# A gated conv FFN behind block-causal attention: the first step of decoding the weights moves to ScalarE, its clamp then reads adjacent words, and the whole order is written anew

## Chip, cores and metric

One core of a Trainium2 chip. The metric is the device time of one execution in microseconds; lower is better. Three runs of the kernel before gave 648.29, 649.46 and 650.03 us (median 649.46).

## What is computed

For 8 batches, 8 heads, 576 positions and a head width of 64, attention with a mask by blocks of 64 positions, and behind it an FFN with a 3-tap convolution along the sequence that gates its own hidden layer. The weights arrive as float64 and are handed to the kernel as pairs of 32-bit words.

```python
scores = q @ k.T / 8, masked where pos_i // 64 < pos_j // 64
attn = exp(scores - max); attn /= sum(attn) + 1e-9
x = (attn @ v), heads side by side                # [8, 576, 512]
h = maximum(x @ w_in, 0)                          # w_in 512 x 1024
conv_out = conv_w[0]*h[t-1] + conv_w[1]*h[t] + conv_w[2]*h[t+1]
out = (h * sigmoid(conv_out)) @ w_out             # w_out 1024 x 512
```

## The kernel before

Everything is one program for one core, without loops at run time. The functions do not issue instructions where they stand: each calls `pl.op(engine, length, function, target, deps, bufs, other=...)`, which only notes an operation, its planned length and, in `other`, further engines that could do it. There are 3677 such operations. At the end `Plan.order` is given the numbers of `TARGETS`, one for each operation in the order of their creation: a number divided by 4 is the operation's place in its engine's queue, and its remainder by 4 chooses the engine (0 the first way, 1 to 3 one of `other`). `order` then walks through a model of the five engines with the planned lengths and settles two more things by it: which of the eight PSUM banks a tile gets, and where TensorE is given filler matmuls (`work`, L1775 in the profile) because its planned idle time is longer than 0.4 us. What runs on the chip is therefore a fixed queue for each engine; nothing is chosen at run time, and an engine that waits holds everything behind it in its queue.

The work has two parts. In the first, batch 0 is computed in two passes over the queries (A: positions 0 to 255, B: the rest), with scores by f32 matmuls (`stage_sa`, L1334, and `stage_sb`, L1273), row maxima on VectorE (L1352, L1289), exponentials on ScalarE (L1360, L1292), the division by the row sum on GpSimd (`norm`, L1375 for 128 and 256 columns, L1310 for 384 and 512), transposes on TensorE (`stage_x`, L1408), their copies out of PSUM on ScalarE (L678) and the product with v (`stage_pv`, L1452). At the same time the weights are loaded and decoded: 16 blocks of 128 x 512 (`load_w`, 8 of w_in and 8 of w_out) and one of 24 x 128 (`load_conv`). In the second part the batches 1 to 7 follow, with attention by `stage_s` (scores L1109, maxima L1208, exponentials L1211, planes L1058 to L1080, product L1492) while the FFN of the batch before runs (`ffn`: first product L1545, relu L1564, taps L1570 to L1587, tanh L1590, gate L1593, planes L1597 to L1604, second product L1638, scaling L1648 and store L1656).

`decode` turns the pairs of words of a float64 into a float32 and is what the change edits. A raw tile holds the words as [128, 512, 2], so word 1, `words(1)`, of neighbouring numbers lies 8 bytes apart, while the result `g` is adjacent. Its four steps are

```python
s1: g = min(words(1) * 2**-112, limit)               # GpSimd or VectorE, L884
s2: words(0) = words(0) >> 29                        # VectorE, L889
s3: words(0) = (words(1) & sign) | words(0)          # VectorE, L892
s4: g = (g << 3) | words(0)                          # VectorE, L897, needs s1 and s3
```

`load_w` calls it with `pool` true for blocks 1 to 15, so that s1 is planned on GpSimd with `c_pool(512) + 0.05`, which is 0.64 us; block 0 and the taps have s1 on VectorE. Behind `decode` come the block's maximum (L921 on VectorE before, for w_in; L924 on ScalarE behind, for w_out), the common scale (`scale_w`, `sums`) and the split into two f16 planes (`split_w`, L952 to L961). The loads of the blocks are issued by SyncE, in its queue among those of q, k and v.

In `Plan.order` a result of one engine reaches an operation of another one `DRAIN + SIGNAL` later (VectorE to VectorE: 0.08 us, the drain alone, before the change).

Of the kernel before, what the change touches and what calls it, by code (L numbers as in the profile page):

```python
# [21 lines left out]
0 12 8 4 0 16 20 8 4 28 24 32 60 80 129 84 196 68 81 64 77 252 128 88 272 284 300 12 36 20 32 60 12 40 18 40 48 0 12 4 8 16 24 44 92 56 100 104 128 72  # L22
204 80 168 184 192 52 120 60 108 156 288 92 244 108 224 248 264 76 208 100 176 260 292 108 268 136 316 324 412 128 320 152 396 416 428 328 336 348 356
368 176 140 388 400 408 420 424 276 472 268 436 197 480 185 516 288 528 189 520 324 560 316 588 144 204 548 616 624 444 132 200 456 488 500 332 140
208 580 596 604 440 156 216 536 556 608 432 160 240 564 696 756 548 184 276 684 700 708 508 172 232 620 644 792 576 180 268 764 784 796 580 816 316
512 820 828 836 844 325 848 616 880 612 864 604 872 628 892 624 896 608 860 600 852 4 56 28 48 32 68 36 44 20 84 88 52 48 40 44 28 24 72 16 52 48 184
304 0 40 56 64 60 52 44 28 48 124 132 68 72 88 84 32 36 120 44 124 68 216 352 8 136 92 96 104 80 112 76 116 212 232 132 124 120 116 26 104 200 84 168
112 220 380 52 240 196 280 204 220 172 236 180 344 364 172 180 168 164 36 36 88 148 264 136 248 160 280 460 452 916 196 200 204 208 212 216 328 364
576 584 420 632 257 653 164 168 172 180 184 188 296 300 524 552 368 568 245 248 220 224 236 240 244 248 348 352 572 600 416 612 436 252 252 256 260
268 272 280 408 464 664 692 492 704 504 288 284 288 292 300 304 308 388 428 628 636 452 648 460 272 320 324 328 332 336 340 396 448 656 660 472 676  # L30
281 284 344 364 368 372 376 380 424 512 736 744 536 760 313 801 384 388 392 396 404 412 468 476 712 720 516 740 544 304 600 608 612 616 620 624 632
636 680 217 348 352 20 112 64 116 68 140 148 96 76 28 152 88 144 84 180 188 92 104 32 160 164 172 100 108 200 216 112 73 56 116 60 132 64 136 76 156
148 80 160 40 96 72 144 92 96 188 372 100 308 208 312 212 332 340 156 160 56 228 140 256 164 276 296 148 144 124 384 392 404 256 260 440 448 192 64
104 120 132 240 120 228 176 312 304 192 308 128 244 116 224 228 232 340 532 152 432 292 444 284 492 508 224 228 108 360 236 376 252 464 496 220 212
156 468 504 512 336 344 540 544 236 194 112 124 316 392 276 360 348 404 400 360 412 296 376 264 356 400 408 456 668 144 484 384 476 372 592 640 260
264 456 728 520 732 524 748 752 296 300 416 680 672 688 496 500 716 724 292 140 148 152 432 488 480 552 468 528 532 472 540 420 480 496 564 504 508
596 840 440 444 448 572 580 584 636 644 912 924 684 940 696 368 516 520 524 532 536 568 648 660 920 936 700 964 373 376 424 428 436 548 552 556 877
656 904 928 688 944 361 364 484 488 492 604 640 644 708 720 984 988 732 1000 385 1013 452 460 464 540 560 564 640 728 996 1004 736 1016 393 396 312
352 356 576 588 628 668 712 976 980 724 992 381 388 528 592 596 648 652 656 704 740 1024 1028 748 1044 401 404 660 664 668 672 676 684 716 744 1040
1048 760 1064 772 440 728 732 740 744 748 756 768 772 832 840 700 704 708 716 720 724 776 780 1157 253 688 692 696 792 796 800 804 808 876 361 448 444  # L40
96 153 100 177 136 233 176 381 768 320 544 856 868 948 344 884 16 20 0 476 776 556 788 568 772 560 780 572 712 1036 756 1032 752 1052 1056 500 808 592
804 584 812 588 824 832 328 336 340 412 416 420 408 428 432 424 793 436 1062 1072 765 1068 665 960 332 908 240 228 232 4 768 1080 236 274 168 164 824
928 1284 633 888 12 24 8 680 968 808 972 780 1020 804 1008 788 760 1128 820 1124 828 1148 1152 736 1096 800 1084 796 1076 784 1116 1120 813 825 456
464 1186 484 460 849 1177 468 476 1201 853 1204 845 1196 817 1136 452 1144 272 264 268 473 1208 276 322 192 196 836 964 1344 653 900 788 1216 892 1180
868 1172 884 1220 896 784 1164 888 1168 880 905 1244 764 1160 856 1140 860 1132 836 1188 1192 488 492 496 917 1266 520 1254 921 512 508 925 516 504
1260 1270 1288 873 1236 865 1212 292 280 288 952 1316 296 308 224 220 848 1028 1428 933 1348 188 485 200 621 204 673 208 677 932 356 752 1088 1100
1104 816 1272 936 1248 944 1280 948 1276 940 828 1312 960 1304 956 1328 1332 812 1228 900 1224 912 1232 908 1256 1292 524 528 532 1342 548 552 1374
556 1381 969 973 544 540 1368 536 1360 1302 1324 1298 1308 308 300 312 1004 1396 316 778 244 248 876 1068 1464 1092 952 956 880 884 888 892 896 900
1088 1092 1500 1096 592 1112 1516 1125 1529 860 864 872 904 908 912 1497 1100 1508 1104 596 1120 1524 604 608 852 856 868 916 920 924 1505 1108 1512
1116 600 1132 1532 1542 616 928 932 936 940 944 948 1521 1136 1536 1128 612 1156 1560 1570 1581 952 956 960 964 968 972 1144 1148 1556 1152 620 1172  # L50
1588 1193 628 980 984 988 992 996 1000 1565 1184 1608 1176 632 1212 1624 640 1641 1004 1008 1012 1016 1020 1024 1188 1196 1612 1200 636 1216 1636 644
676 1056 1060 1064 1068 1072 1076 1665 1256 1688 1252 680 1276 1712 1281 684 1032 1036 1040 1100 1108 1112 1128 1132 1304 401 1048 1052 1088 1092 1096
1124 1144 1148 1340 417 1152 1156 1160 1164 1168 1172 1176 1180 1372 429 1200 1204 1208 1212 1216 1220 1224 1236 1961 461 1228 1232 1244 1248 1252
1256 1260 1264 1464 485 977 1404 840 1364 1008 1376 1012 1400 1020 1356 1000 832 1388 1016 1320 996 1412 1416 820 1336 980 1352 984 1240 988 993 1384
# [77 lines left out]
3336 3340 3344 3348 3352 3536 3540 4460 4468 3552 4476 1813 1816 3356 3360 3364 3368 3380 3384 3556 3560 4484 3564 1820 3576 4492 3581 1828 3448 3452  # L132
3456 3460 3464 3468 3596 3604 4516 4524 3608 4532 4538 4541 3424 3428 3432 3436 3440 3444 4501 3592 4504 4508 3600 4512 4522 4529 3416 3420 3488 3528
3532 3540 3548 3564 4549 1028 3480 3484 3496 3500 3504 3508 3524 3544 4545 1024 3472 3476 3512 3516 3552 3556 3560 3588 3612 1032 3404 3408 3412 3536
3568 3576 3584 3596 3616 3621 3492 3572 3580 3604 3608 3612 3636 3640 3628 3633 3520 3592 3600 3616 3620 3624 3628 3632 3624 1036
"""


# [1730 lines left out]
```

## Time and profile before

| | |
|---|---|
| median of three runs | 649.46 us (648.29 to 650.03) |
| the profiled execution, its own time | 652.3 us |
| span of its instructions | 650.5 us |
| mean granted TensorE clock over the span | 0.982 of full |
| busy share: TensorE, VectorE, ScalarE, GpSimd | 93%, 85%, 74%, 59% |

The profiled execution is 2.8 us above the median of the runs, and 1.8 us of its time lie outside the span. Busy time of TensorE contains stretches at half the clock and the fillers, so a busy TensorE is not always one that gets on with the work. Times of day in the profile are microseconds from the start of the span.

### The profile page before, as it was taken

Reading aid. Unit: us, or ns where it says so; the run is one execution under the profiler, and the core shown is the slowest. Engines: PE = TensorE matmul, PEld = TensorE weight load, DVE = VectorE, ACT = ScalarE, POOL = GpSimd, SP = SyncE. Lnnn points to the kernel's source line nnn. Section 1 sums busy time; section 2 is a strip of 40 time slices with the busy share of each in tenths; the row PEclk is TensorE's granted clock in tenths of the full one; section 3 lists DMA queues with packets and bytes.
Section 4 is the critical chain, followed back from the end, with each engine's and each line's share of the span. In section 5 each row is a group of like instructions: output and inputs, shape, how many; then the busy total and the mean of one; then the engine's idle time right before and its main releaser. Section 6 shows DMA issues by size and latency. Waiting matters only on the chain. (4 is left out here: it accounts for less than half of the span.)

```text
span 650.5 us, 15481 instructions
## 1 busy us (share of the span) xinstructions
PE 606.0 (93%) x5813; PEld 375.1 (58%) x5813; DVE 552.9 (85%) x1148; ACT 481.2 (74%) x1223; POOL 383.3 (59%) x465
## 2 busy tenths in 40 slices
PE   7787889988999999999999999999998999999997
PEld 5444645345874557645674557555755567566654
DVE  7689789999799998999989898989989896974850
ACT  4687789788797967998798676778877667972631
POOL 4978764665277524995587536873677445751320
PEclk9689889999999999999999999999999999999999
DMA  8744213399945999479984599359946662486002
GB/s 300 284 158 158 87 41 98 58 257 195 223 110 140 221 198 173 94 164 213 218 191 78 130 237 226 102 122 208 195 90 142 150 138 59 86 132 154 1 1 81
DMA packets 205503, 96.19 MB, mean 148 GB/s; under 512 B 185308, under 2 KB 187636, under 8 KB 205428
## 3 DMA queue, kind: packets, MB, share of 16 engines
q1 hardware_dynamic: 203844, 92.59, 63.7%
q10 hardware_dynamic: 1584, 2.62, 1.4%
q8 instruction: 45, 0.74, 0.5%
q14 instruction: 30, 0.25, 0.1%
HBM read 39.87 MB, written 9.44 MB: 76 GB/s over the span
## 5 line engine op out<-in xcount | busy, mean ns | idle before, releaser
L1638 PE MATMUL banks<-woh,shared 128*128 128x512 f16 (+1 forms) x592 | 183.5, 374 | 3.1 <-DVE t L1593 1.2
L1545 PE MATMUL banks<-x,wih 128*128 128x288 f16 (+2 forms) x1024 | 158.8, 289 | 8.0 <-DVE t L1593 2.1
L1638 PEld LDWEIGHTS <-shared 128*128 128x128 f16 x888 | 82.7, 98 | 110.1 <-issue 22.4
L1545 PEld LDWEIGHTS <-wih 128*128 128x128 f16 x1024 | 98.5, 99 | 42.5 <-issue 15.1
L1208 DVE TENSOR_REDUCE su<-banks 128x1 f32<-128x384 f32 (+8 forms) x252 | 110.1, 476 | 2.2 <-PE banks L1109 1.7
L1638 PE MATMUL banks<-wol,shared 128*128 128x512 f16 (+1 forms) x296 | 110.5, 373 | 0.0
L1587 POOL TENSOR_TENSOR t<-t,shared 128x575 f32<-128x575 f32 x51 | 75.2, 1477 | 53.5 <-DVE t L1574 50.4
L1109 PE MATMUL banks<-k,q 64*64 64x64 f32 (+7 forms) x1120 | 88.8, 415 | 7.6 <-DVE x L1503 2.8
L1545 PE MATMUL banks<-x,wil 128*128 128x288 f16 (+2 forms) x512 | 86.7, 288 | 0.0
L1604 POOL TENSOR_TENSOR shared<-t,shared 128x576 f16<-128x576 f32 (+2 forms) x53 | 65.4, 1237 | 17.8 <-ACT shared L1597 10.6
L1492 PEld LDWEIGHTS <-vb 128*64 128x64 f16 x1848 | 61.7, 111 | 11.1 <-issue 11.0
L1109 PEld LDWEIGHTS banks<-k,q 64*64 64x64 f32 x1120 | 38.7, 132 | 43.1 <-issue 10.6
L1574 DVE SCALAR_TENSOR_TENSOR t<-banks,cwb,t 128x575 f32<-128x575 f32 (+2 forms) x72 | 53.4, 742 | 10.5 <-ACT t L1570 6.6
L1590 ACT ACTIVATE t<-t 128x576 f32<-128x576 f32 (+2 forms) x72 | 45.1, 630 | 20.1 <-POOL t L1587 13.5
L1593 DVE SCALAR_TENSOR_TENSOR t<-t,banks 128x576 f32<-128x576 f32 (+2 forms) x72 | 48.8, 680 | 11.5 <-ACT t L1590 10.8
L1545 PEld LDWEIGHTS <-wil 128*128 128x128 f16 x512 | 49.8, 98 | 15.1 <-issue 1.7
L1570 ACT ACTIVATE t<-banks,cwb 128x576 f32<-128x576 f32 (+2 forms) x72 | 48.9, 682 | 7.6 <-DVE banks L1567 3.4
L1211 ACT ACTIVATE p3f<-banks,su 128x512 f32<-128x512 f32 (+1 forms) x56 | 36.7, 659 | 9.0 <-DVE su L1208 7.6
L1583 ACT ACTIVATE shared<-banks,cwb 128x575 f32<-128x575 f32 x51 | 37.5, 735 | 4.7 <-DVE banks L1567 4.0
L1211 ACT ACTIVATE p2f<-banks,su 128x320 f32<-128x320 f32 (+1 forms) x56 | 30.9, 554 | 11.0 <-DVE su L1208 9.8
L1648 ACT ACTIVATE stage<-banks,osc 128x512 f32<-128x512 f32 (+1 forms) x29 | 19.3, 669 | 25.3 <-PE banks L1638 23.1
L1564 ACT ACTIVATE banks<-banks 128x576 f32<-128x576 f32 (+2 forms) x50 | 28.1, 565 | 12.7 <-PE banks L1545 12.3
(202 smaller groups left out, 1199.2 us busy)
## 6 DMA issues: line engine op xcount, KB each, us to landing
vn<-in_v_dram SPq DMA_DIRECT2D x32, 320.0 KB, 3.8
q<-in_q_dram SPq DMA_DIRECT2D x28, 320.0 KB, 3.6
k<-in_k_dram SPq DMA_DIRECT2D x28, 320.0 KB, 3.6
out_dram<-stage SPq DMA_DIRECT2D x26, 256.0 KB, 3.2
shared<-in_moe_w_in_dram SPq DMA_DIRECT2D x8, 512.0 KB, 6.9
shared<-in_moe_w_out_dram SPq DMA_DIRECT2D x8, 512.0 KB, 3.4
out_dram<-stage ACTq DMA_DIRECT2D x9, 256.0 KB, 3.4
q<-in_q_dram SPq DMA_DIRECT2D x4, 192.0 KB, 5.6
```

The costliest lines, as they stand in the source:

```text
L1109: nc.tensor.matmul(out[64 * y:64 * y + 64], t["q"].ap[64 * r:64 * r + 64, q0:q0 + 64], t["k"].ap[64 * r:64 * r + 64, k0:k0 + c1 - c0], sta ...
L1208: nc.vector.tensor_reduce(out=st.ap[:, k:k + 1], in_=home[hh].ap[:, x], op=ALU.max, axis=AX.X, negate=True)
L1211: nc.scalar.activation(out=y.ap[:, 0:n], in_=home[hh].ap[:, x], func=AF.Exp, bias=st.ap[:, k:k + 1], accum_out=st.ap[:, 9 + k:10 + k])
L1492: nc.tensor.matmul(y, vb.ap[:, w, c, j, :], x, start=first, stop=(z == 1 and c == jobs[-1][0]), skip_group_check=True)
L1545: nc.tensor.matmul(h(a, z), wt[:, c, fs], xs[c][xi].ap[:, x0 + a:x0 + z], start=(n + c - c0 == 0), stop=(n + c - c0 == 3 * NCC - 1))
L1570: nc.scalar.activation(out=t.ap[:, 0:no], in_=h(own, own + no), func=AF.Copy, scale=cwb.ap[:, NFC + f:NFC + f + 1])
L1574: nc.vector.scalar_tensor_tensor(out=t.ap[:, i0:no], in0=h(own + i0 - 1, own + no - 1), scalar=cwb.ap[:, f:f + 1], in1=t.ap[:, i0:no], op0 ...
L1587: nc.gpsimd.tensor_tensor(out=t.ap[:, 0:i1], in0=t.ap[:, 0:i1], in1=u.ap[:, 0:i1], op=ALU.add)
L1590: nc.scalar.activation(out=t.ap[:, 0:no], in_=t.ap[:, 0:no], func=AF.Tanh)
L1593: nc.vector.scalar_tensor_tensor(out=t.ap[:, 0:no], in0=t.ap[:, 0:no], scalar=1.0, in1=h(own, own + no), op0=ALU.add, op1=ALU.mult)
L1604: eng.tensor_tensor(out=g[1][:, f, carry:carry + no], in0=t.ap[:, 0:no], in1=g[0][:, f, carry:carry + no], op=ALU.subtract)
L1638: nc.tensor.matmul(fb.ap[:, 0:cut], g[a][:, f, cs], w[:, f, ds], start=(f == 0 and n == 0), stop=(f == NFC - 1 and n == 2))
```

## The change

`decode` gets a step s0 ahead of s1, on ScalarE: it reads the words 8 bytes apart, multiplies by 2**-112, takes the absolute value and writes `g`. s1 then works on `g` in place, on adjacent words, as a clamp: a minimum with the limit and a maximum with 0. All 17 calls of `decode` have the same form, with s1 on GpSimd or, as the other way, on VectorE. In `Plan.order` the wait between two operations of one engine other than TensorE gets `SIGNAL` added (VectorE 0.035, ScalarE 0.035, GpSimd 0.08 us). And all of `TARGETS` is replaced: 3694 numbers, 17 more than before, found by a search with six sets of lengths.

```diff
-    def decode(words, g, n, at, deps, bufs, pool):
+    def decode(words, g, n, at, deps, bufs):
+        def s0():
+            nc.scalar.activation(out=g(), in_=words(1).bitcast(F32), func=AF.Abs, scale=2.0 ** -112)
         def s1(eng=nc.gpsimd):
-            eng.tensor_scalar(out=g(), in0=words(1).bitcast(F32), scalar1=2.0 ** -112, scalar2=2.0 ** -96 * (1 + 0x6FFFFF / 2.0 ** 23),
-                              op0=ALU.mult, op1=ALU.min)
+            eng.tensor_scalar(out=g(), in0=g(), scalar1=2.0 ** -96 * (1 + 0x6FFFFF / 2.0 ** 23), scalar2=0.0, op0=ALU.min, op1=ALU.max)
...
-        dv = (DVE, c_dve(n, True), partial(s1, nc.vector), True)
-        a = pl.op(POOL, c_pool(n) + 0.05, s1, at, deps=deps, bufs=bufs, other=(dv,)) if pool else \
-            pl.op(dv[0], dv[1], dv[2], at, deps=deps, bufs=bufs, port=True)
+        a = pl.op(ACT, c_act(n, False) + 0.035, s0, at, deps=deps, bufs=bufs)
+        a = pl.op(POOL, c_pool(n) + 0.05, s1, at, deps=[a], bufs=bufs, other=((DVE, c_dve(n, True), partial(s1, nc.vector), True),))
...
-                lat = self.DRAIN[e] + (self.SIGNAL[c.eng] if c.eng != e else 0.0) if (e != PE or c.eng != PE) else 0.0
+                lat = self.DRAIN[e] + self.SIGNAL[c.eng] if e != PE or c.eng != PE else 0.0
...
-        o = decode(words, lambda: g.ap, 512, at, [ld], [raw, g], f > 0)
+        o = decode(words, lambda: g.ap, 512, at, [ld], [raw, g])
...
-        o = decode(lambda w: raw.ap[:, :, w], lambda: g.ap, P, CONV + 1, [ld], [raw, g], False)
+        o = decode(lambda w: raw.ap[:, :, w], lambda: g.ap, P, CONV + 1, [ld], [raw, g])
```

By the remainders of the new numbers, 476 operations run on another engine than before. Up to batch 0's FFN it is 32 of 755, and VectorE's queue there gets 3 operations longer, ScalarE's 15 longer (17 of them s0), while GpSimd's keeps its 95. From batch 1 on it is 444 of 2922: VectorE has 30 operations fewer, GpSimd 24 more, ScalarE 13 more, and 7 stores fewer are issued by SyncE. s1 is on GpSimd for all 16 blocks of weights, and on VectorE for the taps.

## Rows read from the trace of the kernel before

**Rows 1.** The page, part 1: busy time and share of the span, instructions.

```profile
PE 606.0 (93%) x5813; PEld 375.1 (58%) x5813; DVE 552.9 (85%) x1148; ACT 481.2 (74%) x1223; POOL 383.3 (59%) x465
```

**Rows 2.** Stretches: length, busy PE, PEld, DVE, ACT, POOL, clock, DMA share, GB/s.

```profile
0.00:16.00 16.00, 12.67 (x77) 8.88 (x77) 12.29 (x42) 7.33 (x26) 7.29 (x21) 1.00 0.88 298
16.00:36.00 20.00, 13.18 (x78) 7.97 (x80) 14.03 (x37) 13.98 (x44) 19.15 (x20) 0.74 0.65 238
36.00:60.00 24.00, 22.26 (x165) 13.23 (x166) 21.57 (x64) 21.07 (x59) 18.81 (x20) 0.93 0.55 184
60.00:72.00 12.00, 8.57 (x59) 6.64 (x57) 8.38 (x21) 6.62 (x19) 11.39 (x10) 0.72 0.16 57
72.00:98.00 26.00, 21.44 (x158) 11.79 (x156) 23.22 (x55) 21.51 (x66) 17.14 (x19) 0.93 0.25 79
98.00:130.00 32.00, 29.92 (x180) 15.03 (x181) 31.00 (x67) 26.16 (x63) 18.59 (x30) 1.00 0.32 80
130.00:178.00 48.00, 43.32 (x539) 28.85 (x537) 43.03 (x103) 38.69 (x115) 22.30 (x40) 1.00 1.10 225
178.00:634.00 456.00, 441.73 (x4490) 275.02 (x4489) 397.84 (x763) 343.47 (x834) 268.68 (x312) 1.00 0.68 142
```

**Rows 3.** TensorE's timeline, first 72 us: start, length, what, idle time before and releaser.

```profile
20.10 0.37 PE L1408 MATMUL banks<-rident,p0r 128*128 128x128 f32 x1 [2.71 <-ACT p3f L1292]
21.10 0.49 PE L1408 MATMUL banks<-rident,p1r 128*128 128x128 f32 x2 [0.63 <-POOL p1f L1375]
...
25.55 0.37 PE L1408 MATMUL banks<-rident,p0r 128*128 128x128 f32 x1 [1.43 <-POOL p0f L1375]
...
33.72 0.28 PE L1408 MATMUL banks<-rident,p0r 128*128 128x128 f32 x1 [0.60 <-POOL p0f L1375]
...
35.62 0.33 PE L721 MATMUL banks<-dg,ones_v 128*128 128x128 f32 x1 [1.45 <-POOL dg L717]
...
61.64 0.53 PE L1408 MATMUL banks<-rident,p3r 128*128 128x128 f32 x4 [0.88 <-POOL p3f L1310]
...
65.18 0.75 PE L1408 MATMUL banks<-rident,p3r 128*128 128x128 f32 x4 [2.56 <-POOL p3f L1310]
```

**Rows 4.** GpSimd's timeline around those gaps, same columns.

```profile
14.45 4.50 POOL L884 TENSOR_SCALAR shared<-shared 128x512 f32<-128x512 f32 x2
...
19.67 0.37 POOL L1375 TENSOR_SCALAR p0f<-p0f,st 128x128 f32<-128x128 f32 x1
...
22.12 1.96 POOL L884 TENSOR_SCALAR shared<-shared 128x512 f32<-128x512 f32 x1
...
25.13 0.37 POOL L1375 TENSOR_SCALAR p0f<-p0f,st 128x128 f32<-128x128 f32 x1
...
61.67 2.02 POOL L884 TENSOR_SCALAR shared<-shared 128x512 f32<-128x512 f32 x1
63.78 1.35 POOL L1310 TENSOR_SCALAR p3f<-p3f,st 128x512 f32<-128x512 f32 x1
```

**Rows 5.** Line 884, decode's first step: ns min/median/max, first and last start.

```profile
L884 POOL TENSOR_SCALAR shared<-shared x15: 1949/1967/2460, 14.4 to 81.9; 128x512 f32<-128x512 f32 x15
```

**Rows 6.** The same 20 matmuls of line 1452 on TensorE's timeline, at two clocks.

```profile
35.88 3.96 PE L1452 MATMUL banks<-ptbh,vn 128*64 128x320 f32 x20
...
56.86 2.27 PE L1452 MATMUL banks<-ptbh,vn 128*64 128x320 f32 x20
```

**Rows 7.** Line 1310, the division by row sums on GpSimd, in place and adjacent.

```profile
L1310 POOL TENSOR_SCALAR p3f<-p3f,st x8: 694/728/1347, 25.5 to 91.6; 128x512 f32<-128x512 f32 x8
```

**Rows 8.** Line 924, an absolute value with a sum over 512 columns on ScalarE.

```profile
L924 ACT ACTIVATE junk<-shared x8: 616/629/630, 58.5 to 95.9; 128x512 bf16<-128x512 f32 x8
```

**Rows 9.** The page, part 6: loads of w_in, KB each, us from issue to landing.

```profile
shared<-in_moe_w_in_dram SPq DMA_DIRECT2D x8, 512.0 KB, 6.9
```

**Rows 10.** Waits of VectorE from 14 to 100 us: total, times, longest.

```profile
DVE shared L897 <- POOL shared L884: 3.0, 2, 2.5
```

**Rows 11.** Fillers of line 1775 alone, by stretch: length, busy PE and PEld, clock.

```profile
130.00:178.00 48.00, 8.84 (x35) 6.35 (x35) 1.00 1.10 225
```

229 rows, old and new, of the table TARGETS are left out of this document.

## The prediction

> **What bounds the kernel now.** I began with the page's busy shares: TensorE is busy 93% of the span and no other engine over 85% [rows 1]. A share over the whole span mixes stages, so the next view is the table of stretches [rows 2]. Subtract busy from length and read the clock beside it. From 178 to 634 us TensorE is idle for 456.00 - 441.73 = 14.3 us, at full clock: that part is bound by TensorE, and little can be won there. From 16 to 98 us it is idle for 6.8 + 1.7 + 3.4 + 4.6 = 16.5 us, and the clock falls to 0.74 and 0.72 in the two stretches where the idle share is largest. In those two GpSimd is busy 19.15 of 20.00 us and 11.39 of 12.00 us, more than any other engine: there it is the bound, though its share of the span is the smallest.
>
> Next, what ends TensorE's gaps. Seven of them in the first 72 us, 2.71 + 0.63 + 1.43 + 0.60 + 1.45 + 0.88 + 2.56 = 10.3 us, end at once behind an operation of GpSimd; six name one, the first names an exponential on ScalarE [rows 3]. GpSimd's timeline shows why it was late: the norm of 0.37 us that opens the transposes at 20.10 starts at 19.67 and has two steps s1 of 4.50 us in its queue ahead of it; that at 25.13 has one of 1.96 us ahead; the norm at 63.78, behind the gap of 2.56 us, stands directly behind one of 2.02 us [rows 4]. An s1 takes 1967 ns, and the 15 of them start between 14.4 and 81.9 us [rows 5]. The plan prices it at 0.64 us, so norms meant to be ready come some 1.3 us late for each s1 ahead of them.
>
> The low clock makes this dearer. The same 20 matmuls took 3.96 us at 35.88 and 2.27 us at 56.86 [rows 6]: two levels, half speed (1.2 GHz) for most of the first and full speed (2.4 GHz) in the second, and the low one follows the gaps. Lost work is length times (1 - clock): 20 x 0.26 + 24 x 0.07 + 12 x 0.28 + 26 x 0.07 = 12.1 us [rows 2].
>
> **Step 1: s1 becomes a clamp of adjacent words on GpSimd.** The trace has no minimum or maximum on adjacent words there. Nearest row: line 1310, same engine, same 128x512 f32, in place, two operations by scalars, adjacent: 728 ns [rows 7]. The other end is s1 as it stands, 1967 ns, should the minimum and not the step of 8 bytes be what is slow; a second comparison could take it above that. I take 0.73 us, because the form differs from line 1310 only in the operations, while s1 today differs in the distance of its words as well. GpSimd then spends 16 x 0.73 = 11.7 us where it spent 15 x 1.967 = 29.5 us, 17.8 us less, with one clamp more (block 0 comes over from VectorE).
>
> Here a rule speaks against the change. The row says 1967 / 512 = 3.8 ns for each element 8 bytes apart, against 1.4 ns for adjacent ones [rows 5, 7]. The Trainium skill, GPSIMD Engine Reference, section "Performance pitfalls for Q7 kernels", puts the cliff for reads at a step of more than 8 bytes, which int32 passes only beyond a step of two; s1 steps by exactly two words, so by that page the distance costs nothing, the 1967 ns belong to the operation, and the clamp keeps them. The trace cannot separate the two; the rule is the first rival.
>
> What this takes from the path: the six gaps that name GpSimd sum to 7.55 us; each has at least one s1 ahead in the queue and shrinks by up to 1.24 us for each, so I take 70%, 5.3 us. The first gap ends with ScalarE and GpSimd almost together, and I take half of it, 1.3 us. Sum -6.5 us, bounds 0 and -10.3. VectorE's 3.0 us of waiting for s1 [rows 10] go too, and lie beside these gaps. What is late next is ScalarE's exponential, as the first gap shows, and then VectorE, which has 6.0 + 2.4 + 3.6 + 2.8 = 14.8 us of idle time from 16 to 98 us [rows 2]. Its own work there is almost unchanged (3 operations more), so 14.8 us is a ceiling for all that this stage can give.
>
> **Step 2: the clock.** With shorter gaps TensorE stays at the high level for longer. The two worst stretches hold 5.2 + 3.4 = 8.6 us of lost work. Part of it would only turn into waiting for VectorE; I take a little under a third, -2.5 us, bounds 0 and -8.6.
>
> **Step 3: s0 on ScalarE.** 16 blocks at 629 ns, the row of an absolute value over 512 columns [rows 8], and about 0.3 us for the taps: 10.4 us. That row reads adjacent words; a step of 8 bytes on ScalarE stands in no row, and the bounds are 0.63 and, by the ratio that s1 shows today, 1.7 us. I take the low end, since nothing on ScalarE's rows departs from its columns. ScalarE idles for 98 - (7.33 + 13.98 + 21.07 + 6.62 + 21.51) = 27.5 us up to 98 us [rows 2], which is the cover. It is not complete: an s0 in the queue holds the exponentials behind it, and their row sums and norms, for its length, and if its block has not landed (6.9 us from issue [rows 9]) for longer. I take a fifth of the 10.4 us, +2 us, bounds 0 and +5. s0 and the clamp in a row take 0.63 + 0.73 = 1.36 us with one hand-over between, less than 1.97 us, so s4 is not later.
>
> **Step 4: the new order.** In the first part only 32 of 755 operations change engines, so it stays the same stage with shorter s1. From batch 1 on 444 of 2922 do, and VectorE loses 30 operations, at the mean of 552.9 / 1148 = 0.48 us about 14 us [rows 1]. From 178 us on that is worth little, since TensorE bounds it. From 130 to 178 us TensorE's 4.7 us of idle time [rows 2] and 35 fillers of 8.84 us [rows 11] show it waiting for other engines; the few of the 30 that fall there help. I take -1 us, bounds -4 and +4: the 14.3 us of idle time late in the kernel can shrink or grow by a quarter. The longer wait in the plan changes no instruction; it acts only through fillers and banks, and the fillers stand in idle time. Seven stores that leave SyncE's queue for ScalarE's are issue time of its sequencer in a part where ScalarE idles over 110 us; nothing.
>
> **Sum.** -6.5 - 2.5 + 2 - 1 = -8 us. Against the profiled execution that is 652.3 - 8 = 644.3 us; it stood 2.8 us above the median of the runs, and runs are what is measured, so 649.5 - 8 = **641.5 us**, 1.2% less. A measurement of this kernel tells about 0.3%, 2 us, from no change.
>
> **Rivals.** *The clamp is as slow as s1.* Then GpSimd has 16 x 1.967 = 31.5 us instead of 29.5, all gaps stay, and ScalarE's steps come on top: 649.5 + 2 (one more clamp, where GpSimd is the bound) + 2 - 1 = 652.5 us, slower. Steps 1 and 2 give 9 us for 1.24 us saved on each clamp; with +2 - 1 to pay, it decides from a clamp of about 1.8 us. For it: min stands on GpSimd nowhere else in the trace. Against it: the step of 8 bytes does not stand there elsewhere either, and line 1310 does two operations in 0.73 us. 12%.
>
> *VectorE and ScalarE take the gaps over.* VectorE is busy 21.57 of 24.00 us from 36 to 60 us and 31.00 of 32.00 us from 98 to 130 us [rows 2]; if its idle 14.8 us before that are waits for loads and for its own chains, GpSimd's relief ends as GpSimd's idle time: 649.5 - 2 + 2 - 1 = 648.5 us, no change that can be told. Against it: in both stretches with the lowest clock VectorE is busy only 70% of the time. 10%.
>
> *The new order misses later.* If moving 444 operations adds 10 us to the 14.3 us of idle time after 178 us, it eats the first part's gain: 649.5 - 9 + 2 + 10 = 652.5 us, slower. Against it: VectorE, the busiest behind TensorE, gets lighter there. 3%.
>
> **Numbers.** The forecast's case has 75%, all of it faster by over 0.3% (below 647.5 us). Its own range reaches from 634 us, where steps 1 and 2 give half as much again and step 3 little, to 647.5 us. Taking in the second rival brings the upper end to 650 us; past it lie the first and third, and below 634 us a twentieth, some 2 in 10 together. Faster 0.75, same 0.11 (the second rival and a little of the third's spread), slower 0.14.
>
> **What would show it.** Right: line 884's successor on GpSimd at 0.7 to 0.8 us, 16 times; s0 on ScalarE at 0.6 to 0.65 us; GpSimd busy some 18 us less before 98 us; the seven gaps under 4 us together; a clock above 0.85 from 16 to 36 us; the FFN's first product (line 1545) some us sooner; VectorE's share up in that stage. Wrong: a clamp near 2 us; s0 near 1.2 us; gaps of the same length that now name ScalarE or VectorE; or a gain at 98 us that is gone at 634 us.

## The result, and the profile after

The changed kernel takes 628.25 us, median of 4 runs (627.96 to 629.15); the kernel before, run beside it, 648.88 us (647.67 to 650.03). The ratio is 0.9685 with a 95% interval of 0.9663 to 0.9707: faster by 20.6 us, where 8 us had been forecast and 634 us was the low end of the range. The direction was right and the size far too small.

The page of the changed kernel, part 1 and the clock line of part 2, answers to [rows 1]:

```profile
PE 595.4 (95%) x5814; PEld 372.7 (60%) x5814; DVE 532.0 (85%) x1121; ACT 490.0 (78%) x1243; POOL 375.9 (60%) x489
...
PEclk9999999999999999999999999999999999999999
```

VectorE is 20.9 us lighter than before and executes 27 instructions fewer, yet its share is the same, because the span shrank with it. No slice of the clock line is under 9 now.

The table of stretches, columns as in [rows 2]; the last row ends at 610 us, since the span does at 626.1 us:

```profile
0.00:16.00 16.00, 12.52 (x73) 8.44 (x75) 10.60 (x39) 8.92 (x31) 6.37 (x22) 1.00 0.86 304
16.00:36.00 20.00, 15.99 (x119) 9.62 (x117) 19.79 (x53) 18.85 (x57) 13.99 (x23) 1.00 0.70 246
36.00:60.00 24.00, 21.05 (x176) 14.85 (x175) 23.87 (x69) 23.95 (x66) 16.54 (x21) 1.00 0.59 204
60.00:72.00 12.00, 10.98 (x83) 6.74 (x81) 11.91 (x28) 11.83 (x31) 9.53 (x14) 1.00 0.34 113
72.00:98.00 26.00, 22.86 (x165) 13.29 (x164) 24.94 (x61) 25.88 (x70) 13.47 (x19) 1.00 0.25 77
98.00:130.00 32.00, 29.78 (x217) 12.96 (x217) 30.98 (x81) 24.08 (x70) 18.83 (x32) 1.00 0.58 133
130.00:178.00 48.00, 43.84 (x544) 33.38 (x540) 42.30 (x87) 39.64 (x101) 28.10 (x38) 1.00 1.07 202
178.00:610.00 432.00, 425.53 (x4382) 266.13 (x4380) 366.83 (x712) 333.82 (x820) 269.08 (x325) 1.00 0.71 146
```

Three things are to be seen beside [rows 2]. The clock is 1.00 where it was 0.74 and 0.72. From 16 to 98 us VectorE idles 0.21 + 0.13 + 0.09 + 1.06 = 1.5 us instead of 14.8: VectorE has become the bound of this stage. ScalarE is nearly as full, but the run without s0 below shows that it does not hold the stage up; GpSimd has fallen back. And behind 178 us TensorE idles 432.00 - 425.53 = 6.5 us where it idled 14.3: the part that the prediction held to be settled has changed too. (The two rows do not hold quite the same work, since the changed kernel is some 14 us further on at 178 us; the cut below compares the same work.)

TensorE's timeline from 14 to 76 us, all of its gaps over 0.4 us, columns as in [rows 3]:

```profile
18.72 0.28 PE L1410 MATMUL banks<-rident,p0r 128*128 128x128 f32 x1 [0.72 <-POOL p0f L1377]
...
21.12 0.28 PE L1410 MATMUL banks<-rident,p0r 128*128 128x128 f32 x1 [0.71 <-POOL p0f L1377]
...
25.86 0.49 PE L1777 MATMUL banks<-rident 128*128 128x512 f32 x1 [1.00 <-ACT p3f L1294]
...
30.30 0.25 PE L1410 MATMUL banks<-rident,p0r 128*128 128x128 f32 x1 [0.91 <-POOL p1f L1377]
...
37.03 0.54 PE L1410 MATMUL banks<-rident,p3r 128*128 128x128 f32 x4 [0.56 <-POOL p3f L1312]
...
43.24 0.30 PE L722 MATMUL banks<-dg,ones 128*128 128x128 f32 x1 [0.67 <-ACT p4f L1139]
...
56.29 0.42 PE L1410 MATMUL banks<-rident,p2r 128*128 128x128 f32 x3 [1.18 <-DVE x L1464]
...
69.28 0.42 PE L1410 MATMUL banks<-rident,p2r 128*128 128x128 f32 x3 [0.80 <-DVE t L1595]
...
74.52 0.72 PE L1547 MATMUL banks<-x,wih 128*128 128x322 f16 x4 [0.92 <-ACT p4f L1139]
```

The gaps behind GpSimd fell from 7.55 us [rows 3] to 0.72 + 0.71 + 0.91 + 0.56 = 2.9 us. What remains names all three engines, none longer than 1.2 us.

The two new steps, by their lines (ns min/median/max, first and last start), answer to [rows 5]:

```profile
L885 ACT ACTIVATE shared<-shared x16: 668/681/722, 8.9 to 72.8; 128x512 f32<-128x512 f32 x16
...
L888 POOL TENSOR_SCALAR shared<-shared x16: 610/617/1066, 9.7 to 73.6; 128x512 f32<-128x512 f32 x16
```

The clamp takes 617 ns where s1 took 1967, and the last one starts at 73.6 us instead of 81.9.

To see where the 20.6 us lie, the span is cut at one event that all kernels have, the start of the first relu of batch 1's FFN on ScalarE. In the changed kernel's timeline it is

```profile
162.85 0.63 ACT L1566 ACTIVATE banks<-banks 128x576 f32<-128x576 f32 x1
```

and in that of the kernel before it started at 176.98 us. So 14.1 us were won up to it, and the rest of the span went from 650.5 - 177.0 = 473.5 to 626.1 - 162.8 = 463.3 us. The rest, of the kernel before and of the changed one, columns as in [rows 2]:

```profile
177.00:650.40 473.40, 455.64 (x4577) 283.50 (x4575) 400.34 (x767) 346.76 (x840) 269.22 (x312) 1.00 0.67 140
```
```profile
162.85:626.10 463.25, 452.73 (x4575) 284.00 (x4573) 379.71 (x731) 351.31 (x853) 281.25 (x335) 1.00 0.70 145
```

TensorE's idle time there fell from 473.40 - 455.64 = 17.8 to 463.25 - 452.73 = 10.5 us, its busy time by 2.9 us.

The table uses this cut for every kernel that was timed; the experiments are described below it. "Ratio" is to the kernel before, run on the same chip. The median is taken over all runs of a kernel, the event and the rest from its one profiled execution, and they scatter more. The profiled execution of before took 652.3 us, 3.4 us above the median, and two later traces with the slow s1 and (but for a few of the moved operations of one of them) the old queues reach the event at 174.6 and 172.7 us. "Changed, old wait" has the queues and the median of the changed kernel, yet its event comes 2.8 us later and its rest is as much shorter. So differences of up to about 3 us in the last two columns, and some 3 us of the 14.1 us, may be scatter.

| kernel | median us | ratio, 95% interval | event at, us | rest, us |
|---|---|---|---|---|
| before | 648.88 | 1 | 177.0 | 473.5 |
| changed | 628.25 | 0.9685 [0.9663, 0.9707] | 162.8 | 463.3 |
| decode alone, old order | 643.18 | 0.9917 [0.9887, 0.9947] | 169.4 | 473.9 |
| new order, old s1 | 640.76 | 0.9884 [0.9845, 0.9924] | 175.6 | 464.2 |
| adjacent words, same s1 | 649.17 | 1.0002 [0.9974, 1.003] | 174.6 | 474.0 |
| new order, minimum first | 643.24 | 0.9904 [0.9869, 0.9939] | 177.1 | 461.6 |
| both steps on GpSimd | 635.17 | 0.9788 [0.975, 0.9827] | 169.3 | 462.9 |
| the same, w_out alone | 634.55 | 0.9775 [0.9739, 0.9812] | 168.5 | 464.2 |
| changed, no s0 | 628.72 | 0.9692 [0.9657, 0.9727] | 163.7 | 464.9 |
| changed, old wait | 628.3 | 0.9676 [0.9636, 0.9715] | 165.7 | 460.4 |
| changed, thirty back | 636.25 | 0.9808 [0.976, 0.9855] | 163.1 | 470.6 |
| before, thirty off | 648.96 | 1.0005 [0.9982, 1.0028] | 172.7 | 474.6 |
| changed, swap | 630.0 | 0.9727 [0.9688, 0.9766] | 161.8 | 464.6 |
| changed, half back | 632.6 | 0.9743 [0.9707, 0.978] | 162.4 | 464.7 |

### The profile page after: what moved, and what is told of

It reads as the page before. It is cut to its first block, busy times and chain, and to the rows that moved or that the text cites. A ratio compares the mean times of both kernels' runs of the same rounds, so it can differ in the third digit from the quotient of the medians.

```text
span 626.1 us, 15524 instructions
## 1 busy us (share of the span) xinstructions
PE 595.4 (95%) x5814; PEld 372.7 (60%) x5814; DVE 532.0 (85%) x1121; ACT 490.0 (78%) x1243; POOL 375.9 (60%) x489
## 4 chain that ended last, share of the span: by engine, by line
PE 45%; DVE 29%; ACT 13%; POOL 6%; DMA 4%; issue 3%; SPq 1%; ACTq 0%; POOLq 0%; DVEq 0%
PE banks L1640 19%; PE banks L1547 13%; DVE su L1210 6%; PE banks L1494 6%; PE banks L1111 6%; DVE ptbl L1066 3%; DVE t L1595 2%; DVE t L1576 2%; DVE ptbm L1066 2%; POOL t L1589 2%; POOL shared L1606 2%; DMA vn<-in_v_dram 2%; DVE vb L834 1%; ACT t L1592 1%; DVE h L1066 1%
## 5 line engine op out<-in xcount | busy, mean ns | idle before, releaser
L1547 PE MATMUL banks<-x,wih 128*128 128x288 f16 (+2 forms) x1024 | 155.4, 286 | 6.4 <-DVE t L1595 2.8
L1210 DVE TENSOR_REDUCE su<-banks 128x1 f32<-128x192 f32 (+8 forms) x252 | 110.2, 476 | 1.2 <-ACT p2f L1213 0.3
L1111 PE MATMUL banks<-k,q 64*64 64x512 f32 (+7 forms) x1120 | 86.6, 414 | 3.2 <-DVE x L1505 1.8
L1606 POOL TENSOR_TENSOR shared<-t,shared 128x576 f16<-128x576 f32 (+2 forms) x53 | 64.3, 1215 | 24.3 <-ACT shared L1599 14.1
L1576 DVE SCALAR_TENSOR_TENSOR t<-banks,cwb,t 128x575 f32<-128x575 f32 (+2 forms) x72 | 53.3, 743 | 18.6 <-ACT t L1572 13.7
L1213 ACT ACTIVATE p2f<-banks,su 128x384 f32<-128x384 f32 (+1 forms) x56 | 30.8, 553 | 4.4 <-DVE su L1210 3.6
```

The source lines that it names most:

```text
L1111: nc.tensor.matmul(out[64 * y:64 * y + 64], t["q"].ap[64 * r:64 * r + 64, q0:q0 + 64], t["k"].ap[64 * r:64 * r + 64, k0:k0 + c1 - c0], sta ...
L1210: nc.vector.tensor_reduce(out=st.ap[:, k:k + 1], in_=home[hh].ap[:, x], op=ALU.max, axis=AX.X, negate=True)
L1213: nc.scalar.activation(out=y.ap[:, 0:n], in_=home[hh].ap[:, x], func=AF.Exp, bias=st.ap[:, k:k + 1], accum_out=st.ap[:, 9 + k:10 + k])
L1547: nc.tensor.matmul(h(a, z), wt[:, c, fs], xs[c][xi].ap[:, x0 + a:x0 + z], start=(n + c - c0 == 0), stop=(n + c - c0 == 3 * NCC - 1))
L1576: nc.vector.scalar_tensor_tensor(out=t.ap[:, i0:no], in0=h(own + i0 - 1, own + no - 1), scalar=cwb.ap[:, f:f + 1], in1=t.ap[:, i0:no], op0 ...
L1606: eng.tensor_tensor(out=g[1][:, f, carry:carry + no], in0=t.ap[:, 0:no], in1=g[0][:, f, carry:carry + no], op=ALU.subtract)
```

## The experiments

### The two halves of the change by themselves

**Decode alone.** The kernel before with its own numbers, queues and banks; s0 is issued on ScalarE some 0.9 us of planned time ahead of its s1, and s1 is the clamp.

```diff
-            eng.tensor_scalar(out=g(), in0=words(1).bitcast(F32), scalar1=2.0 ** -112, scalar2=..., op0=ALU.mult, op1=ALU.min)
+            eng.tensor_scalar(out=g(), in0=g(), scalar1=..., scalar2=0.0, op0=ALU.min, op1=ALU.max)
...
+            while j < i and line[j].start < o.start - 0.9:
+                j += 1
+            early.setdefault(j, []).append(firsts[o.seq])
```

> The kernel before with its plan, queues, banks and fillers as they are; only decode is edited: s0 goes into ScalarE's queue about 0.9 us of planned time ahead of each s1, and s1 is the clamp. Theory A (GpSimd's slow s1 holds the first part; its relief brings the first part's gain in any order): the first part, up to the last first-product group of batch 0, loses 8 to 13 us, the granted clock from 16 to 36 us is above 0.9, the time is 636 to 641 us, and what comes behind 104 us is as long as before. Theory B (the new order brings nearly all, decode alone only moves the waits to ScalarE): 645 to 650 us, with gaps of TensorE in the first 72 us that still sum to over 8 us.

**The new order alone.** The changed kernel, in which s0 issues nothing and s1 is the old multiplication and minimum on words 8 bytes apart.

```diff
         def s0():
-            nc.scalar.activation(out=g(), in_=words(1).bitcast(F32), func=AF.Abs, scale=2.0 ** -112)
+            pass
...
```

> The changed kernel with the new order, but s0 issues nothing and s1 on GpSimd is the old one that multiplies and limits words 8 bytes apart. Theory A: s1 takes 1.97 us again, 16 times, GpSimd is busy some 20 us more up to 98 us, the first part gives back 9 to 15 us, and the time is 637 to 643 us; the later part stays as short as in the changed kernel. Theory B: the new order hides the slow s1, 628 to 633 us.

Measured: the decode alone 0.9917, which is -5.6 us against the runs beside it; the order alone 0.9884, -8 us. The order alone came out as theory A had it. The decode alone lies between the ranges of its two theories: the clock from 16 to 36 us is 0.83, not above 0.9, and TensorE's gaps of 0.4 us and more from 14 to 72 us sum to 6.5 us, not to over 8. Two of these gaps are the only one over 0.5 us there that names GpSimd, and the longest:

```profile
30.89 0.45 PE L721 MATMUL banks<-dg,ones_v 128*128 128x128 f32 x1 [0.71 <-POOL dg L717]
...
54.24 0.38 PE L1550 MATMUL banks<-x,wih 128*128 128x256 f16 x2 [1.41 <-ACT ptbh L678]
```

Together the two halves are worth 20.6 us, some 7 more than the sum. The table says where: the order alone takes 9.3 us off the rest and next to nothing off the first part (-1.4 us by these two traces, and nothing against the two later ones named above); the decode alone takes 7.6 us off the first part and nothing off the rest. By these traces 14.1 - 1.4 - 7.6 = 5.1 us of the surplus, most of it, lie in the first part. One row each of the table of stretches shows what it is, 16 to 98 us, of the changed kernel, of the decode alone, and of the order alone:

```profile
16.00:98.00 82.00, 70.88 (x536) 44.50 (x535) 80.50 (x206) 80.51 (x221) 53.52 (x75) 1.00 0.47 161
```
```profile
16.00:98.00 82.00, 68.99 (x511) 42.06 (x511) 74.21 (x194) 77.98 (x220) 50.34 (x73) 0.96 0.44 149
```
```profile
16.00:98.00 82.00, 64.14 (x459) 39.59 (x455) 68.31 (x177) 61.70 (x180) 70.06 (x69) 0.90 0.42 148
```

VectorE (third busy time) idles 82 - 80.50 = 1.5 us with both, 7.8 us with the decode alone, 13.7 us with the order alone, 14.8 us before. With the slow s1 neither order fills it; with the fast one in the old queues half of it stays; the new queues take the rest. Which of the moved operations do so was not tried.

### What made s1 slow

**Adjacent words, same operations.** In the kernel before, s1 of blocks 1 to 15 reads a constant with adjacent words instead of words(1); the real weights of these blocks are left out.

```diff
-            eng.tensor_scalar(out=g(), in0=words(1).bitcast(F32), ...)
...
+                x = ones.bitcast(F32).unsqueeze(1).broadcast_to([P, 4, P])
...
+                eng.tensor_scalar(out=y, in0=x, scalar1=2.0 ** -112, scalar2=lim, op0=ALU.mult, op1=ALU.min)
```

> The kernel before, old order, no s0; s1 of blocks 1 to 15 reads an adjacent constant in place of the block's words, with the same two operations, so the weights are not the reference's. It shows GpSimd's relief without ScalarE's extra steps. Theory A: s1 takes 0.6 to 0.8 us, the time is 634 to 640 us, 0 to 3 us below the run with decode alone (that difference is what s0 costs in the old order). Theory B: 645 to 650 us. If the operation and not the distance is slow, s1 stays near 1.97 us and the time near 649 us.

Its line on GpSimd:

```profile
L891 POOL TENSOR_SCALAR shared<-ones x15: 1917/1922/2434, 14.3 to 81.5; 128x512 f32<-128x512 f32 x15
```

1922 ns on adjacent words against 1967 [rows 5], and the time is that of before. The theory that the distance of the words is what makes s1 slow fell.

**Four forms side by side.** The kernel before, profiled once; each of blocks 1 to 15 has one of four forms of s1: multiply and minimum, or minimum and maximum, on words 8 bytes apart or adjacent. The correct decoding of most blocks is left out.

> The kernel before, with four kinds of s1 on GpSimd by block number: multiply and minimum on words 8 bytes apart (blocks 4, 8, 12), minimum and maximum on words 8 bytes apart (1, 5, 9, 13), multiply and minimum on an adjacent constant (2, 6, 10, 14), minimum and maximum on an adjacent constant (3, 7, 11, 15); the weights are therefore not the reference's. If the distance is what costs: 1.9 to 2.0 us for both kinds at 8 bytes and 0.6 to 0.8 us for both adjacent kinds. If the minimum costs (the rival): about 2 us for all four. If both do: four different values.

Four rows of GpSimd's timeline (start, length); `ones` as input is the adjacent one, L891 multiplies, L893 clamps:

```profile
16.53 0.62 POOL L893 TENSOR_SCALAR shared<-ones 128x512 f32<-128x512 f32 x1
...
25.15 0.65 POOL L893 TENSOR_SCALAR shared<-shared 128x512 f32<-128x512 f32 x1
...
26.55 1.95 POOL L891 TENSOR_SCALAR shared<-shared 128x512 f32<-128x512 f32 x1
...
34.21 1.92 POOL L891 TENSOR_SCALAR shared<-ones 128x512 f32<-128x512 f32 x1
```

The distance costs 0.03 us, the pair of operations 1.30 us. None of the three outcomes that were expected came: two forms are short and two long, by their operations. The rows are among the shortest of three or four of each form; the longest of a short form takes 1.07 us, so the two groups do not meet.

**Minimum first.** The changed kernel without s0, with s1 as a minimum and then a multiplication, one instruction on words 8 bytes apart.

```diff
+            eng.tensor_scalar(out=g(), in0=words(1).bitcast(F32), scalar1=2.0 ** 16 * (1 + 0x6FFFFF / 2.0 ** 23), scalar2=2.0 ** -112,
+                              op0=ALU.min, op1=ALU.mult)
...
```

> The changed kernel, but s0 issues nothing and s1 on GpSimd reads the words 8 bytes apart and takes the minimum first (with the limit times 2**112) and multiplies then; the result is the same. The price run showed 1.92 us for multiply then minimum on adjacent words and 0.65 us for minimum then maximum on words 8 bytes apart, so it is the pair of operations that is slow. Theory P (only a minimum behind a multiplication is slow): s1 takes 0.6 to 0.8 us, ScalarE is 10 us less busy up to 98 us, and the time is 622 to 628 us. Theory Q (any pair of a multiplication with a minimum is slow): s1 takes 1.9 us and the time is that of the new order with the old s1, 639 to 643 us.

It came out at 0.9904, like the new order with the old s1 (theory Q), since the step takes what the old one took:

```profile
L888 POOL TENSOR_SCALAR shared<-shared x16: 1948/1967/2440, 7.2 to 87.3; 128x512 f32<-128x512 f32 x16
```

**Five pairs.** The kernel before, profiled once, with five forms of s1 for the blocks in turn, always 128x512 f32 from words 8 bytes apart; in four of them the limit is left out: L886 minimum and multiply, L888 multiply and maximum, L890 multiply twice, L892 multiply and add, L894 multiply alone.

> The kernel before with five kinds of s1 on GpSimd by block number, all on words 8 bytes apart: minimum then multiply (5, 10, 15), multiply then maximum (1, 6, 11), multiply twice (2, 7, 12), multiply then add (3, 8, 13), multiply alone (4, 9, 14); the weights are not the reference's except in the first kind. Theory P: 0.6 to 0.8 us for all but multiply then maximum, which is 1.9 us like multiply then minimum. Theory Q: 1.9 us for minimum then multiply too. If any multiplication of words 8 bytes apart were slow, all five would be near 1.9 us.

Their lines on GpSimd:

```profile
L886 POOL TENSOR_SCALAR shared<-shared x3: 1985/2015/2301, 25.0 to 75.7; 128x512 f32<-128x512 f32 x3
...
L888 POOL TENSOR_SCALAR shared<-shared x3: 1960/1960/2546, 15.1 to 58.1; 128x512 f32<-128x512 f32 x3
...
L890 POOL TENSOR_SCALAR shared<-shared x3: 644/863/1081, 20.0 to 65.8; 128x512 f32<-128x512 f32 x3
...
L892 POOL TENSOR_SCALAR shared<-shared x3: 642/657/658, 17.0 to 78.5; 128x512 f32<-128x512 f32 x3
...
L894 POOL TENSOR_SCALAR shared<-shared x3: 1519/1536/1951, 27.8 to 63.6; 128x512 f32<-128x512 f32 x3
```

Two comparisons, two multiplications, or a multiplication and an addition take 0.61 to 0.64 us at the least. A multiplication with a comparison, in either order, takes 1.92 us and more (1.95 and more on words 8 bytes apart), as theory Q had it. A multiplication alone takes 1.52 us and more, where both theories had it short. Why is not shown; the pairs are.

### Where the first step should stand

**Both steps on GpSimd.** The changed kernel; for the 16 blocks ScalarE's step issues nothing, and GpSimd does a multiplication with an added zero right ahead of the clamp.

```diff
...
+            if own:
+                eng.tensor_scalar(out=g(), in0=words(1).bitcast(F32), scalar1=2.0 ** -112, scalar2=0.0, op0=ALU.mult, op1=ALU.add)
+            eng.tensor_scalar(out=g(), in0=g(), scalar1=lim, scalar2=-lim if own else 0.0, op0=ALU.min, op1=ALU.max)
...
```

> The changed kernel, but the first step runs on GpSimd too: multiply then add 0 on words 8 bytes apart, directly ahead of the clamp, in the clamp's place in the queue; ScalarE's step issues nothing. By the price runs that is 0.65 + 0.62 = 1.27 us a block on GpSimd, and 17 x 0.66 = 11 us less on ScalarE, which was busy 11.83 of 12.00 and 25.88 of 26.00 us from 60 to 98 us. Theory S (ScalarE is the bound there after the change): 622 to 627 us. Theory G (the norms on GpSimd still set the pace, so that 10 us more on it in this order cost): 630 to 636 us.

**The same for the eight blocks of w_out alone.**

> The changed kernel, with the first step as multiply then add on GpSimd for the 8 blocks of w_out alone, which fall into the stretch where ScalarE is full, and on ScalarE for the others. Theory S: 623 to 627 us. Theory G: 629 to 633 us.

**No s0 at all.** The changed kernel without s0 and without the limit (that part of the computation is left out): s1 is two multiplications, 0.64 us at the least and 0.73 at the median.

> The changed kernel without s0 and without the clamp: s1 on GpSimd multiplies twice on words 8 bytes apart, which the price run showed at 0.64 us. It leaves out the limit for weights too large for a float32. It shows what ScalarE's extra step costs in this order, as GpSimd's share stays as it is. Step 3 of the prediction (+2 us for s0): 625 to 627.5 us. Theory S (ScalarE, at 99% in this stretch, is the bound): 618 to 624 us. If VectorE, at 97%, is the bound and ScalarE beside it hidden: 627 to 629 us.

The first two lose 7 and 6 us: theory G, though the second, 634.55 us, lies past the 633 us that it allowed. The eight steps of w_out alone cost nearly as much as all 16; why was not tried. The third equals the changed kernel, 0.9692 against 0.9685, as it should with VectorE as the bound. Row 16 to 98 us of both steps on GpSimd, then of no s0:

```profile
16.00:98.00 82.00, 67.44 (x498) 42.15 (x491) 75.71 (x193) 67.53 (x192) 64.79 (x88) 0.94 0.44 152
```
```profile
16.00:98.00 82.00, 71.30 (x535) 45.04 (x535) 79.97 (x205) 74.14 (x209) 55.42 (x74) 0.98 0.48 166
```

16 short steps more on GpSimd, 11 us, leave VectorE idle again for 82 - 75.71 = 6.3 us and bring the clock down to 0.94. Taking s0 away, on the other hand, frees ScalarE, 80.51 to 74.14 us, and nothing happens: VectorE stays full at 79.97 of 82 us.

### What the order does behind batch 1's first relu

**The old wait.** The changed kernel with the planner's old line for waits within an engine: only banks and fillers can differ.

> The changed kernel with the old line for the wait within an engine in its plan. The queues are the same, since the numbers fix them; only fillers and banks can differ. Theory (the wait matters only through the search that wrote the numbers): 627 to 630 us, the same within 0.3%. Rival (fillers and banks that the longer wait places bring part of the gain, most of it before 178 us): 632 us or more.

0.9676 against 0.9685: this edit alone does nothing that shows.

**Thirty back.** The changed kernel, with 30 operations of batches 1 to 7 that the new order took from VectorE (26 subtractions `h2p`, 4 copies `evh`) issued there again, each at its planned place.

```diff
+    back = [868, 1000, 1229, ...]
+    back = {i: [w[2] for w in ((pl.ops[i].eng, 0, pl.ops[i].fn),) + tuple(pl.ops[i].other) if w[0] == DVE][0] for i in back}
     for o in pl.order(...):
-        o.fn()
+        back.get(getattr(o, "seq", None), o.fn)()
```

> The changed kernel with 30 operations of batches 1 to 7 given back to VectorE at the place in time where the plan has them (26 subtractions of line 1082 from GpSimd, 4 copies of line 1499 from ScalarE), so that VectorE has as many operations as before. Theory C (the later part's 9 to 10 us come from VectorE being lighter): 633 to 638 us, all of the loss behind the first relu of batch 1. Theory D (they come from the order of the queues, which is finer than the load): 627 to 631 us.

**Thirty off.** The converse: the kernel before, with the same 30 taken from VectorE.

> The kernel before, with its own order and its own decode; only the same 30 operations of batches 1 to 7 that the previous run gave back to VectorE (26 subtractions h2p and 4 copies evh) are here taken from VectorE and issued by GpSimd (26) and ScalarE (4), at their planned places. Theory C (in the later part VectorE's load is what the new order lightens, and that is most of its gain there): the part behind the second FFN pass, 473.5 us in the kernel before, falls by about the 7 us that it rose by when the operations were given back, to 465 to 468 us, TensorE's idle time there from 17.8 to about 12 us, and the total to about 642 us; the first part stays at 177 us. Rival O (the gain needs the new queues: in the old ones GpSimd and ScalarE have other work at those places, and a subtraction is late there as often as VectorE is now free): the later part stays at 472 to 475 us and the total at 647 to 651 us.

Part 1 of the page of thirty back, then of thirty off:

```profile
PE 598.8 (94%) x5814; PEld 373.4 (59%) x5814; DVE 541.6 (85%) x1151; ACT 487.5 (77%) x1239; POOL 359.8 (57%) x463
```
```profile
PE 603.3 (93%) x5813; PEld 373.5 (58%) x5813; DVE 542.5 (84%) x1118; ACT 483.0 (75%) x1227; POOL 398.7 (62%) x491
```

Given back, the 30 add 541.6 - 532.0 = 9.6 us to VectorE and 7.3 us to the rest, 463.3 to 470.6 us, while the first part keeps its time; by the medians the loss is 8.0 us (theory C). Taken off in the old queues they relieve VectorE by 552.9 - 542.5 = 10.4 us, and the rest stays at 474.6 us: no gain at all (rival O). So VectorE's load is not by itself what bounded the old order. Either it counts only in queues that are built for it, or any operation off its planned place costs time. The next two are to tell these apart.

What ended TensorE's waits from 178 to 600 us (total us, times, longest): the first rows of the list, of the kernel before, of thirty off, and of the changed kernel with its last row.

```profile
PE banks L1545 <- DVE t L1593: 2.1, 6, 0.6
PE banks L1545 <- DVE x L1503: 1.9, 1, 1.9
PE banks L1545 <- ACT p4f L1211: 1.9, 2, 1.3
```
```profile
PE banks L1109 <- DVE t L1593: 2.7, 5, 1.3
PE banks L1545 <- DVE t L1593: 2.0, 5, 0.9
PE banks L1545 <- ACT p4f L1211: 1.5, 2, 0.8
PE banks L1545 <- ACT x L1497: 1.5, 1, 1.5
```
```profile
PE banks L1547 <- DVE t L1595: 1.9, 3, 1.5
...
PE banks L1111 <- ACT p4f L1213: 0.3, 1, 0.3
```

Summed over the whole lists, the waits that name VectorE are 7.4 us before, 6.0 with thirty off and 5.1 in the changed kernel; those that name ScalarE, mostly its exponentials, are 5.7, 8.0 and 0.3 us. Thirty back has 8.6 and 2.5 us. So taking the 30 off in the old queues shortened the waits behind VectorE and lengthened those behind ScalarE, and what the new order nearly did away with is the waits behind ScalarE. Which operations make the exponentials come in time was not tried.

**Swap, and half back.** Swap: 13 of the subtractions go back to VectorE, and 13 others that the new order keeps there go to GpSimd. Half back: only the first 13 move.

> The changed kernel with 26 subtractions h2p of batches 1 to 7 on another engine than planned, each at its planned place: 13 of those that the new order moved off VectorE go back to it, and 13 others that it keeps on VectorE go to GpSimd. VectorE's and GpSimd's loads stay within 2 us, but 26 operations are displaced, about as many as the 30 that were given back. Theory C (VectorE's load is what costs): the part behind the FFN pass of batch 1 stays at 463 to 465 us, total 627 to 630 us. Rival O (displacement itself costs, whatever the loads): that part rises by about as much as with the 30 given back, to 468 to 471 us, total 634 to 637 us.

> The changed kernel with only the first 13 subtractions of the swap given back to VectorE, and no counter-move: half of the load that the 30 operations put on it, half the displacement. Theory C: the part behind the FFN pass of batch 1 rises by about half of 7 us, to 466 to 468 us, total 631 to 633 us, and clearly more than the swap. Rival O: also about half, since 13 operations are displaced, but less than the swap, which displaces 26.

Row 178 to 610 us of swap, then of half back:

```profile
178.00:610.00 432.00, 425.19 (x4373) 265.55 (x4370) 367.12 (x713) 332.74 (x818) 266.36 (x321) 1.00 0.71 146
```
```profile
178.00:610.00 432.00, 424.47 (x4375) 265.48 (x4373) 369.62 (x723) 333.43 (x819) 262.45 (x313) 1.00 0.70 146
```

With 26 operations displaced and VectorE's load unchanged (367.12 against 366.83 us) the rest is 464.6 us and the ratio 0.9727, whose interval overlaps the changed kernel's; displacement of nearly as many operations as in thirty back does not cost what that cost (theory C). Half back, at 0.9743, lies between, about where half of the load should put it. But it was to be clearly slower than the swap, and the two intervals overlap; and its rest, 464.7 us, is that of the swap and not the 466 to 468 us expected. That trace is of its fastest run, 628.99 us, 3.6 us under its median, so the rest says little there. So the medians put most of the loss of thirty back down to VectorE's load, and some 2 us may be displacement; half back does not settle it. That the load explains the gain of the new order is not shown: in the old order a lighter VectorE gained nothing.

## Why the prediction was right and wrong

**Step 1, the clamp: right for a wrong reason.** 0.73 us was forecast, 0.617 measured, and the gaps behind GpSimd lost 4.6 us where 5.3 was the term. (With the decode alone, in the old order, the gaps of 0.4 us and more from 16 to 72 us that name GpSimd came down to 0.7 us.) But the step gave the distance of the words as what sets s1 apart, "s1 today differs in the distance of its words as well", and the runs with adjacent words show that it is the pair of operations. The row of 2 operations in 728 ns [rows 7] was a fair neighbour only by luck: its pair happens not to be a slow one. The Trainium skill, GPSIMD Engine Reference, "Performance pitfalls for Q7 kernels", was right that a step of 8 bytes costs nothing on reads, 0.65 against 0.62 us here. The consequence that the prediction drew from it for its first rival, that the clamp would keep the 1967 ns, did not follow, because minimum with maximum is a fast pair.

**Step 2, the clock: right in sign, its size not measured by itself.** Lost work was 12.1 us; by the same product it is 20 x 0.17 = 3.4 us with the decode alone and 0 in the changed kernel. That is more work regained than the 2.5 us that were forecast as time, but no run shows how much of it became time and how much waiting. Steps 1 to 3 together, forecast as -6.5 - 2.5 + 2 = -7 us, are measured by the decode alone: -5.6 us.

**Step 3, s0: the price right, the charge wrong.** 681 ns against the 629 taken, far from the bound of 1.7. The +2 us for delayed exponentials is not there in the changed kernel: without s0 the time is the same. Its cover is VectorE, which is full beside it. In the old order s0 was not tried by itself; with the decode alone the gaps of 0.4 us and more from 16 to 72 us that name ScalarE sum to 5.4 us, where they summed to 3.4, so part of the +2 us may be there.

**Step 4, the new order: this step failed.** "From 178 us on that is worth little, since TensorE bounds it", -1 us with bounds of 4 either way. The new order is worth 8 us by itself and 15 us on top of the new decode (20.6 - 5.6). The step has two errors, in different places. Behind 178 us the step took TensorE's 14.3 us of idle time as something that could move by a quarter; it went to 6.5 us, and over the same work from 17.8 to 10.5. A busy share of 97% there was read as a bound. The list of the waits that make up most of the missing 3%, from 178 to 600 us and shown in part above, has none over 1.9 us and all but 0.3 us of it behind VectorE or ScalarE: time that another order could take. The 14 us taken off VectorE was worked out in the step and then priced at almost nothing; thirty back prices 9.6 us of it at 7 to 8 us within the new order. In the first part the step said that the order "stays the same stage with shorter s1". The ceiling of 14.8 us of idle VectorE time was worked out correctly and then hardly used: the changed kernel reached it to within 1.5 us, and the old order with the fast step left 7.8 us of it.

**The rivals.** A clamp as slow as s1 fell with the 617 ns, though its premise, that the operations and not the distance set the 1967 ns, was right. That VectorE and ScalarE take the gaps over is what happened in the end (VectorE as the bound), but behind a gain of 14 us instead of 2. The new order missing later had the opposite sign.

## What to carry to other kernels

When a step becomes cheaper and the order is searched again, price the order by the idle time of the engine that will bound next, not by how many operations change engines: the fast step was worth 6 us here, the new order 8, and both together 21. A busy share of 97% does not settle the idle time that is left; ask what ends each gap. And an edit that gives work back and one that takes it away are two experiments: here the first cost 7 to 8 us and the second gained nothing.

## What the runs showed of the hardware that was not expected

On GpSimd one instruction with two operations by scalars, over 128x512 f32, takes 0.62 us or 1.95 us by which two they are: minimum with maximum, multiply with add, and multiply with multiply are the short ones, multiply with minimum or maximum the long ones, and a multiplication alone, 1.52 us at the least, is longer than one with an added zero, 0.64 us. So s1 could be split into two instructions of GpSimd and still be shorter than one. On ScalarE an absolute value into f32 from words 8 bytes apart took 681 ns, 8% over the 629 ns of [rows 8], whose input is adjacent, whose output is bf16 and which adds up a sum; which of these differences it is was not tried.
